# Top-k attention and two MLP layers in one Trainium2 kernel: layers that open with two rows, a 64-token unit moved behind its neighbour, low words of the probabilities made on GpSimd, and one parametric ReLU

## The chip, the core and the metric

The kernel runs on one core of one Trainium2 chip. The metric is the device time of one execution in microseconds (us); lower is better. Durations of single instructions are given in us or, where a row of the trace has them so, in ns. The engines are named as the profile names them: PE (TensorE), DVE (VectorE), ACT (ScalarE), POOL (GpSimd) and SP (the engine that issues most DMAs).

## What is computed

Attention over 4 batches, 8 heads, 576 tokens and 64 channels per head, in which each row of the scores keeps its 32 largest entries, then two MLP layers of 512 to 2048 to 512 channels over all 2304 tokens. Cut to what matters:

```python
scores = (q @ k.T) / 8
kth = np.partition(scores, -32, axis=-1)[..., -32:-31]
scores = np.where(scores >= kth, scores, -1e9)
attn = softmax(scores)                 # 32 entries a row are left
x = (attn @ v).reshape(2304, 512)      # heads side by side
h = np.maximum(x @ w_in1, 0.0);  x = (h * h) @ w_out1
h = x @ w_in2;                   out = np.maximum(0.01 * h, h) @ w_out2
```

## The kernel before, in words

**Numbers.** Most products are made of a high word (the operand rounded to PE's one-pass format, `R`) and a low word (the rest). A layer's hidden row needs 12 matmuls: four channel chunks of high weights by high x, four of high weights by low x, four of low weights by high x. The attention of the first `NATIVE` = 3 units is multiplied in full fp32 instead (line 405, two PE records a matmul); of all later units the probabilities are split in two words.

**Attention.** Two heads are worked on together, a *head pair* (`hp`, 4 of them). `UNITS` (line 27) lists pieces of a batch: (batch, first token, tokens). A unit by a head pair gives score tiles of 128 rows by 576 keys; 144 tiles in all, handled in 72 *pairs of tiles*. The program is written slot by slot, 16 slots to a pair of tiles (loop at line 831): in slots 0 to 13 DVE finds the 32 largest of both tiles, with four MAX8 (line 846) and three MATCH_REPLACE8 (line 848) a tile; around them `at(slot, function)` puts the other steps: loads, scores (line 285, copied from PSUM by ACT in line 286), the exponentials (lines 303 and 307), the normalisation on POOL (line 316), the four transposes of a tile (line 321) and its leftover columns (line 334). `pt_main` (line 318) copies a transposed tile out of PSUM: ACT writes the high word (line 326) and DVE subtracts it from the PSUM tile for the low word (line 327). `av_split` (line 408) multiplies with V, 9 matmuls a head (line 416); `x_out` (line 424) writes x of the MLP as two words. Scores of batches 2 and 3 (`EARLY`) are computed ahead of their turn as filler for PE in the first part, stored to DRAM (`sd`) and loaded back.

**MLP.** The 2304 tokens are cut into `BLOCKS` of 512, 256, 384, 512, 256 and 384. `moe(j, layer)` (line 570) runs one layer of one block in 16 steps `f` of 128 hidden channels: a hidden row of 12 matmuls into the PSUM tile `h`, of which there is one (line 585), the activation, its high word `gh` (ACT) and low word `gl` (POOL, for the last block DVE), and one step later the second product into the `acc` tiles (four of them; lines 635 and 637). The first layer's square takes ACT, ACT and POOL (lines 602 to 604). The second layer's leaky ReLU takes two ACT passes and a POOL subtraction (lines 613 to 615), for the last block one ACT pass and a DVE maximum (lines 609, 610). At the end of a first layer ACT and DVE turn each of the four `acc` tiles into the next layer's x, high word `xh` and low word `xl` (lines 648, 649); the second layer's first row waits for these. At the end of a second layer ACT copies the result to `y`, two buffers, and stores it (lines 652, 654). Layers come in the order (block, layer) 00, 01, 10, 11, 20, 21, 30, 31, 40, 50, 41, 51; weights are read as 64-bit numbers and split into two words during block 0 (`w_convert_steps`, lines 512 to 533), stored to DRAM, and loaded from there by the later blocks.

**What sets the order.** `moe` is a generator. Between attention slots the loop at line 831 lets it run by `rate` quanta, which is a block's number of quanta over the slots until the next block's x is complete (`rslot`, line 773). The framework then orders each engine's instructions by a simulated timeline, in which the attention's functions rank 100 places ahead (`SOON`). On the chip each engine runs its own list in that fixed order.

## Time and profile before

| what | value |
|---|---|
| three runs, median (lowest to highest) | 1200.16 us (1199.25 to 1202.18) |
| the profiled execution, its own time | 1201.19 us |
| its span in the trace | 1199.4 us |
| PE busy | 1130.8 us, 94% |
| DVE busy | 945.1 us, 79% |
| ACT busy | 796.4 us, 66% |
| POOL busy | 678.9 us, 57% |
| DMA traffic | 323.24 MB, mean 270 GB/s |

The span runs from the first to the last instruction; 1.8 us of the profiled execution lie around it. A busy PE is not a PE at its peak, since matmuls are pipelined and their recorded durations overlap; where it matters, distances from start to start are used. PEclk is the clock that was granted to PE as a share of its full 2.4 GHz.

### The profile page before, as it was taken

How to read it: one execution, taken by the hardware profiler on the slowest of the kernel's cores; microseconds unless marked ns; L12 is line 12 of the kernel's file. 1: busy time of each engine (PE TensorE's matmuls, PEld its weight loads, DVE VectorE, ACT ScalarE, POOL GpSimd, SP SyncE). 2: the span in 40 equal slices, each digit the busy share in tenths (PEclk: the TensorE clock that was granted, in tenths of full speed). 3: DMA queues.
4: the chain of work that ended last, by engine and by line, in shares of the span. 5: the costliest groups of instructions: out<-in, count | busy, mean ns of one | idle time of the engine just before them, and what ended most of it. 6: DMA issues, size and time to landing. Idle time of an engine off the chain costs nothing.

```text
span 1199.4 us, 20071 instructions
## 1 busy us (share of the span) xinstructions
PE 1130.8 (94%) x6388; PEld 989.3 (82%) x6388; DVE 945.1 (79%) x1944; ACT 796.4 (66%) x1787; POOL 678.9 (57%) x922
## 2 busy tenths in 40 slices
PE   5899958999899999999998999999999999999997
PEld 4777846887677789988998997888788899998896
DVE  7999999879879899999999999999999910110121
ACT  6999979789889977766656676555666653334322
POOL 7967575778788875467665664555455543005200
PEclk9999988999999999999998999999999999999999
DMA  9868565679889888899987888676677589779973
GB/s 309 277 213 266 201 218 214 234 290 338 305 296 326 281 298 288 282 333 369 326 308 251 283 279 265 206 232 221 203 231 232 184 277 369 249 250 345 353 253 124
DMA packets 105914, 323.24 MB, mean 270 GB/s; under 512 B 16977, under 2 KB 25169, under 8 KB 101713
## 3 DMA queue, kind: packets, MB, share of 16 engines
q1 hardware_dynamic: 103168, 317.24, 77.6%
q10 hardware_dynamic: 2640, 4.72, 1.1%
q8 instruction: 52, 0.85, 0.3%
q14 instruction: 54, 0.43, 0.1%
HBM read 254.54 MB, written 67.37 MB: 268 GB/s over the span
## 4 chain that ended last, share of the span: by engine, by line
PE 69%; ACT 10%; DVE 10%; DMA 5%; POOL 3%; issue 2%; ACTq 0%; SPq 0%; POOLq 0%; DVEq 0%
PE h L592 28%; PE acc L637 14%; PE acc L635 14%; DVE m L846 4%; PE att L416 4%; PE att L321 3%; DVE w L848 3%; PE att L405 2%; DMA wraw<-in_w_dram 2%; ACT e L303 1%; DMA kraw<-in_k_dram 1%; ACT e L307 1%; DMA out_dram<-y 1%; ACT s L286 1%; ACT stage L286 1%
## 5 line engine op out<-in xcount | busy, mean ns | idle before, releaser
L592 PE MATMUL h<-xh,wi 128*128 128x512 f32 (+2 forms) x1280 | 351.8, 347 | 8.6 <-ACT ga L602 3.5
L846 DVE MAX8 m<-w 128x8 f32<-128x576 f32 x432 | 313.6, 747 | 1.3
L592 PEld LDWEIGHTS h<-xh,wi 128*128 128x128 f32 x1280 | 227.3, 191 | 37.1 <-ACT ga L602 5.0
L848 DVE MATCH_REPLACE8 w<-m,w 128x576 f32<-128x576 f32 x288 | 213.5, 743 | 0.8
L592 PE MATMUL h<-xl,wi 128*128 128x512 f32 (+2 forms) x640 | 207.1, 342 | 2.7 <-DVE xl L649 2.6
L618 POOL TENSOR_TENSOR gl<-ga,gh 128x512 fp32r<-128x512 f32 (+2 forms) x160 | 163.0, 1019 | 43.3 <-ACT gh L617 38.9
L635 PE MATMUL acc<-gh,wo 128*128 128x512 f32 (+2 forms) x768 | 157.4, 342 | 0.3 <-ACT y L652 0.3
L637 PE MATMUL acc<-wo,gh 128*128 128x512 f32 x576 | 151.9, 398 | 2.5 <-ACT gh L617 2.5
L615 POOL TENSOR_TENSOR ga<-ga,gb 128x512 f32<-128x512 f32 (+2 forms) x80 | 81.5, 1018 | 122.3 <-ACT gb L614 122.3
L635 PEld LDWEIGHTS acc<-gh,wo 128*128 128x128 f32 x768 | 127.1, 189 | 12.4 <-ACT y L652 0.8
L592 PEld LDWEIGHTS h<-xl,wi 128*128 128x128 f32 x640 | 121.4, 191 | 14.9 <-DVE xl L649 4.3
L303 ACT ACTIVATE e<-s,m 128x576 f32<-128x576 f32 x144 | 112.4, 781 | 31.1 <-DVE m L846 24.2
L637 PEld LDWEIGHTS acc<-wo,gh 128*128 128x128 f32 x576 | 103.9, 188 | 22.9 <-ACT gh L617 4.0
L307 ACT ACTIVATE e<-e,nb 128x576 f32<-128x576 f32 x144 | 110.9, 774 | 5.7 <-POOL nb L297 5.5
L604 POOL TENSOR_TENSOR ga<-ga 128x512 f32<-128x512 f32 (+2 forms) x80 | 66.3, 828 | 82.3 <-ACT gh L603 79.6
L846 DVE MAX8 m<-s 128x8 f32<-128x576 f32 x144 | 103.7, 747 | 7.9 <-ACT s L286 5.9
L848 DVE MATCH_REPLACE8 w<-m,s 128x576 f32<-128x576 f32 x144 | 107.0, 743 | 0.6
L321 PE MATMUL att<-ident,e 128*128 128x128 f32 x576 | 88.1, 279 | 18.1 <-ACT e L307 12.8
L321 PEld LDWEIGHTS att<-ident,e 128*128 128x128 f32 x576 | 69.7, 143 | 31.2 <-ACT e L307 17.4
L602 ACT ACTIVATE ga<-h 128x512 f32<-128x512 f32 (+2 forms) x80 | 39.1, 488 | 80.2 <-PE h L592 77.8
L316 POOL TENSOR_SCALAR e<-e,rc 128x576 f32<-128x576 f32 x108 | 79.7, 751 | 16.6 <-DVE rc L312 15.4
L617 ACT ACTIVATE gh<-ga 128x384 fp32r<-128x384 f32 (+2 forms) x112 | 58.6, 523 | 42.2 <-POOL ga L615 32.2
(94 smaller groups left out, 2133.4 us busy)
## 6 DMA issues: line engine op xcount, KB each, us to landing
wi<-wd SPq DMA_DIRECT2D x160, 512.0 KB, 5.2
wo<-wd SPq DMA_DIRECT2D x160, 512.0 KB, 5.4
wraw<-in_w_dram SPq DMA_DIRECT2D x32, 1024.0 KB, 6.6
sd<-stage SPq DMA_DIRECT2D x72, 288.0 KB, 3.3
s<-sd SPq DMA_DIRECT2D x72, 288.0 KB, 4.6
wd<-wi SPq DMA_DIRECT2D x32, 512.0 KB, 5.6
wd<-wo SPq DMA_DIRECT2D x32, 512.0 KB, 6.0
kraw<-in_k_dram SPq DMA_DIRECT2D x16, 576.0 KB, 4.5
```

The costliest lines, as they stand in the source:

```text
L303: ACT.activation(t["e"], t["s"], AF.Prelu, bias=pr["m8"][:, i, 31:32], scale=-1.0, alpha=1.0 / FAR)
L307: ACT.activation(e, e, AF.Exp, bias=pr["nb"][:, i:i + 1], scale=-FAR, accum_out=pr["sum"][:, i:i + 1])
L316: POOL.tensor_scalar(e, e, pr["rc"][:, i:i + 1], 1.0, op0=OP.mult, op1=OP.mult)
L321: PE.transpose(ps[:, j * P:(j + 1) * P], t["e"][:, j * P:(j + 1) * P], ident)
L592: PE.matmul(h[:, 0:n], lhsT=wi[:, w, c * P:(c + 1) * P], rhs=x[c][y][:, 0:n], start=cnt == 0, stop=cnt == 3 * NK - 1)
L604: POOL.tensor_tensor(a[:, 0:n], a[:, 0:n], a[:, 0:n], op=OP.mult)
L615: POOL.tensor_tensor(a[:, 0:n], a[:, 0:n], b[:, 0:n], op=OP.subtract)
L618: (DVE if j >= GLD else POOL).tensor_tensor(gl[:, 0:n], a[:, 0:n], gh.bitcast(F)[:, 0:n], op=OP.subtract)
L635: PE.matmul(acc[c][:, 0:n], lhsT=wo[:, w, cs], rhs=g[:, 0:n], start=first, stop=last)
L637: PE.matmul(acc[c], lhsT=g[:, cs], rhs=wo[:, w, :], start=first, stop=last)
L846: cur["dve"] = DVE.max(out=m8[:, x, 8 * r:8 * r + 8], in_=t["s"] if r == 0 else t["w"])
L848: cur["dve"] = DVE.match_replace(out=t["w"], in_to_replace=m8[:, x, 8 * r:8 * r + 8], in_values=t["s"] if r == 0 else t["w"], imm_value=NEG)
```

## The change

1. `UNITS` has the 64-token unit (0, 512, 64) behind (1, 0, 256), no longer ahead of it, and `NATIVE` falls from 3 to 2, so that this unit's probabilities are split in two words as well. Block 1 (256 tokens) is then the unit (1, 0, 256) alone, and the rate of block 0's MLP is set by 8 pairs of tiles until block 1 is complete, not 10; that of block 1 by 12, not 10. The scores of the moved unit (`KEPT`) are still computed with its batch, stored to DRAM and loaded back.
2. The low word of a transposed tile is made on POOL: ACT copies the PSUM tile a second time, whole, to `whole` (two buffers), and POOL subtracts the high word from that.
3. A layer opens with two hidden rows at once: at step 0 the 24 matmuls of rows 0 and 1 go out in the order `OPENING`, by the x chunk that they need, the second row into a tile of the `acc` kind; step 1 then has no matmuls of its own. The words `xh` and `xl` at a first layer's end rank 400 places ahead (`SEAM`).
4. The second layer's leaky ReLU is one ACT pass with `Prelu`, for all blocks.

```diff
 UNITS = [
-    (0, 0, 256), (0, 256, 256), (0, 512, 64), (1, 0, 256), (1, 256, 320),
+    (0, 0, 256), (0, 256, 256), (1, 0, 256), (0, 512, 64), (1, 256, 320),
     (2, 0, 256), (3, 0, 256), (2, 256, 320), (3, 256, 320),
 ]
+OPENING = (
+    ((0, 0),), ((1, 0),), ((0, 1),), ((2, 0),), ((1, 1),), ((3, 0),), ((2, 1), (3, 1)),
+)
-NATIVE = 3
+NATIVE = 2
+KEPT = 3
+SEAM = 400
...
         if half == 0:
-            if direct(uh):
+            if direct(uh) and not kept(uh):
                 t["s"] = sbufs[t["i"] % NS]
...
-        if half == 1 and not direct(uh):
+        if half == 1 and (kept(uh) or not direct(uh)):
...
         if split(t["uh"]):
             pts = late["PT"]
             ACT.activation(pts[:, 0:4, c:c + P], x, AF.Copy)
-            DVE.tensor_tensor(pts[:, 4:8, c:c + P], x, pts.bitcast(F)[:, 0:4, c:c + P], op=OP.subtract)
+            whole = late["pool"].tile([P, NJ, P], F, tag="whole", name="whole", bufs=2)
+            ACT.activation(whole, x, AF.Copy)
+            POOL.tensor_tensor(pts[:, 4:8, c:c + P], whole, pts.bitcast(F)[:, 0:4, c:c + P], op=OP.subtract)
...
                 if f == 0:
-                    mm = [(w, c, 0) for w in range(2) for c in range(NK)] + [(0, c, 1) for c in range(NK)]
+                    two = [late["psum"].tile([P, 512], F, tag="acc" if r else "h", name="h", bufs=4 if r else 1)
+                           for r in range(2)]
+                    ws = [wi, wt[si + 1][0]]
+                    mm = [(r, w, c, y) for part in OPENING for r in range(2) for c, y in part
+                          for w in ((0,) if y else (0, 1))]
+                elif f > 1:
+                    two = [late["psum"].tile([P, 512], F, tag="h", name="h", bufs=1)]
+                    ws = [wi]
+                    mm = [(0, 0, c, y) for c in range(NK) for y in range(2)] + [(0, 1, c, 0) for c in range(NK)]
                 else:
-                    mm = [(0, c, y) for c in range(NK) for y in range(2)] + [(1, c, 0) for c in range(NK)]
+                    mm = []
...
-                elif j >= LEAK2:
-                    ACT.activation(a[:, 0:n], h[:, 0:n], AF.Copy, scale=0.01)
-                    DVE.tensor_tensor(a[:, 0:n], a[:, 0:n], h[:, 0:n], op=OP.max)
                 else:
-                    b = late["mlp"].tile([P, 512], F, tag="gb", name="gb", bufs=1)
-                    ACT.activation(a[:, 0:n], h[:, 0:n], AF.Relu)
-                    ACT.activation(b[:, 0:n], h[:, 0:n], AF.Relu, scale=-0.01)
-                    POOL.tensor_tensor(a[:, 0:n], a[:, 0:n], b[:, 0:n], op=OP.subtract)
+                    ACT.activation(a[:, 0:n], h[:, 0:n], AF.Prelu, alpha=0.01)
...
             if layer == 0:
                 xh, xl = x[c]
-                ACT.activation(xh[:, 0:n], acc[c][:, 0:n], AF.Copy)
-                DVE.tensor_tensor(xl[:, 0:n], acc[c][:, 0:n], xh.bitcast(F)[:, 0:n], op=OP.subtract)
+                with tc.high_priority(offset=SEAM):
+                    ACT.activation(xh[:, 0:n], acc[c][:, 0:n], AF.Copy)
+                    DVE.tensor_tensor(xl[:, 0:n], acc[c][:, 0:n], xh.bitcast(F)[:, 0:n], op=OP.subtract)
```

Where the change moves instructions, the built programs show it. First PE at the opening of block 2's second layer (384 tokens; `h` is a hidden row, `xh` and `xl` the two words of x, `PTs` and `VT` the attention's product). Before:

```order
L635 MATMUL acc_7093<-gl_8105,wo_7918 128x384
L592 MATMUL h_8184<-xh0_5146,wi_7998 128x384
L416 MATMUL att_8199<-PTs_3112,VT_7982 128x256 x8
L592 MATMUL h_8184<-xh0_5146,wi_7998 128x384 x7
L416 MATMUL att_8199<-PTs_3112,VT_7982 128x256
L592 MATMUL h_8184<-xl0_5147,wi_7998 128x384 x4
L592 MATMUL h_8230<-xh0_5146,wi_8065 128x384
```

and now:

```order
L656 MATMUL acc_7169<-gl_8213,wo_8034 128x384
L436 MATMUL att_8304<-PTs_2609,VT_8078 128x256
L619 MATMUL h_8292<-xh0_5191,wi_8100 128x384 x4
L436 MATMUL att_8304<-PTs_2609,VT_8078 128x256 x8
L619 MATMUL h_8293<-xh0_5191,wi_8169 128x384 x4
L619 MATMUL h_8292<-xl0_5192,wi_8100 128x384
L619 MATMUL h_8293<-xl0_5192,wi_8169 128x384
L619 MATMUL h_8292<-xh0_5191,wi_8100 128x384 x2
L619 MATMUL h_8293<-xh0_5191,wi_8169 128x384 x2
```

The second row (`h_8293`) now stands inside the first, and the last low words of x are needed 24 row matmuls after the opening began, not 12.

The same place on DVE, where `xl` is made from the `acc` tiles among the MAX and MATCH_REPLACE of the attention. Before:

```order
L649 TENSOR_TENSOR xl0_5147<-acc_7090,xh0_5146 128x384
L649 TENSOR_TENSOR xl0_5147<-acc_7091,xh0_5146 128x384
L846 MAX m8_8369<-s4_105 128x8
L846 MAX m8_8369<-s5_106 128x8
L846 MAX m8_8234<-w_8237 128x8
L649 TENSOR_TENSOR xl0_5147<-acc_7092,xh0_5146 128x384
L649 TENSOR_TENSOR xl0_5147<-acc_7093,xh0_5146 128x384
```

and now:

```order
L671 TENSOR_TENSOR xl0_5192<-acc_7166,xh0_5191 128x384
L867 MAX m8_8325<-w_8328 128x8
L671 TENSOR_TENSOR xl0_5192<-acc_7167,xh0_5191 128x384
L671 TENSOR_TENSOR xl0_5192<-acc_7168,xh0_5191 128x384
L867 MAX m8_8325<-w_8329 128x8
L671 TENSOR_TENSOR xl0_5192<-acc_7169,xh0_5191 128x384
```

Two MAX stand between the first and the last `xl`, not three. Counted over DVE's whole list, the MAX between the last `xl` of block 0 and of block 1, of block 1 and of block 2, of block 2 and of block 3 are 88, 96 and 133 before, and 71, 117 and 139 now.

Last, POOL in block 0's first layer, between the low words of weights (`wi`, `wo`), the square (`ga`) and its low word (`gl`). Before:

```order
L533 TENSOR_TENSOR wi_2862<-wc_2864,wi_2862 128x512
L604 TENSOR_TENSOR ga_2970<-ga_2970 128x512
L533 TENSOR_TENSOR wo_2863<-wc_2864,wo_2863 128x512
L618 TENSOR_TENSOR gl_2969<-ga_2970,gh_2968 128x512
L533 TENSOR_TENSOR wi_2934<-wc_2936,wi_2934 128x512
```

and now:

```order
L553 TENSOR_TENSOR wi_2900<-wc_2902,wi_2900 128x512
L639 TENSOR_TENSOR gl_2925<-ga_2926,gh_2924 128x512
L347 TENSOR_TENSOR PTs_2609<-whole_2982,PTs_2609 128x4x128
L631 TENSOR_TENSOR ga_3000<-ga_3000 128x512
L553 TENSOR_TENSOR wo_2901<-wc_2902,wo_2901 128x512
L639 TENSOR_TENSOR gl_2999<-ga_3000,gh_2998 128x512
L347 TENSOR_TENSOR PTs_2609<-whole_3021,PTs_2609 128x4x128
```

The probabilities' low words (`PTs<-whole`) stand in the queue between the MLP's; 8 of them lie between the first `gl` of layer 00 and the first of layer 01, and 112 in the whole list.

## Rows read from the trace of the kernel before

**Rows 1.** Busy time by stretch, cut at openings (316.24:427.69 is layer 01 alone); columns first.

```profile
core 0: us, PE busy (x) PEld busy (x) DVE busy (x) ACT busy (x) POOL busy (x), PEclk, DMA share, GB/s
200.00:316.24 116.24, 111.15 (x560) 92.14 (x558) 99.48 (x191) 98.43 (x197) 91.26 (x98) 0.99 0.80 287
316.24:427.69 111.45, 106.34 (x505) 85.69 (x505) 98.17 (x186) 101.35 (x195) 94.60 (x98) 0.98 0.89 308
316.24:500.61 184.37, 178.44 (x1075) 155.87 (x1076) 169.99 (x336) 154.79 (x327) 134.80 (x165) 0.99 0.87 299
500.61:645.05 144.44, 142.08 (x906) 134.69 (x904) 142.58 (x302) 91.19 (x214) 93.00 (x140) 1.00 0.91 325
645.05:848.37 203.32, 197.65 (x1007) 168.50 (x1007) 199.27 (x421) 122.89 (x262) 112.60 (x154) 0.97 0.76 247
848.37:1010.18 161.81, 161.18 (x956) 140.64 (x956) 114.10 (x239) 93.86 (x199) 84.68 (x110) 1.00 0.73 243
1010.18:1199.40 189.22, 181.95 (x1022) 169.91 (x1020) 30.20 (x56) 63.37 (x141) 24.81 (x34) 0.99 0.78 266
```

**Rows 2.** Busy time in five openings of layers, from first row to second product.

```profile
645.05:657.83 12.78, 9.86 (x43) 8.58 (x44) 12.72 (x28) 6.77 (x16) 4.75 (x9) 0.73 0.64 225
316.24:327.43 11.19, 9.42 (x30) 6.28 (x31) 11.19 (x23) 10.61 (x20) 7.99 (x9) 0.85 0.98 345
736.16:747.27 11.11, 8.37 (x31) 6.02 (x32) 10.98 (x23) 7.23 (x15) 2.54 (x4) 0.85 0.81 251
848.37:858.23 9.86, 9.27 (x41) 6.61 (x41) 9.79 (x20) 7.84 (x16) 2.85 (x5) 1.00 0.59 188
500.61:507.72 7.11, 6.22 (x43) 5.23 (x41) 7.04 (x17) 4.60 (x13) 2.96 (x4) 1.00 0.82 315
```

**Rows 3.** Timeline of PE, opening of block 2's second layer: start, us, engine, line, operation.

```profile
646.28 1.71 PE L592 MATMUL h<-xh,wi 128*128 128x384 f32 x7
650.40 1.15 PE L592 MATMUL h<-xl,wi 128*128 128x384 f32 x2 [1.95 <-DVE xl L649]
652.52 0.69 PE L592 MATMUL h<-xh,wi 128*128 128x384 f32 x1 [0.96 <-ACT gb L614]
```

**Rows 4.** Timeline of ACT, opening of block 3's first layer.

```profile
742.68 0.60 ACT L652 ACTIVATE y<-acc 128x512 f32<-128x512 f32 x1 [2.58 <-DMA out_dram<-y]
743.70 0.60 ACT L602 ACTIVATE ga<-h 128x512 f32<-128x512 f32 x1 [0.42 <-ACT y L652]
```

**Rows 5.** The chain that ended last, in order of time: start, us, what.

```profile
752.12 2.81 PE acc L635 x12
1031.14 2.08 PE h L592 x12
```

**Rows 6.** Groups of DVE, 500.61 to 645.05: count, busy us, mean ns, idle before.

```profile
L846 DVE MAX8 m<-w 128x8 f32<-128x576 f32 x70 | 50.6, 746 | 0.2
L327 DVE TENSOR_TENSOR PTs<-att,PTs 128x512 fp32r<-128x512 f32 x26 | 17.4, 678 | 0.4 <-ACT PTs L326 0.2
```

**Rows 7.** Groups by shape over the span: the operations that leave, move, or price one.

```profile
L326 ACT ACTIVATE PTs<-att 128x512 fp32r<-128x512 f32 x108 | 62.8, 596 | 19.2 <-PE att L321 18.6
L615 POOL TENSOR_TENSOR ga<-ga,gb 128x512 f32<-128x512 f32 x32 | 41.5, 1298 | 20.4 <-ACT gb L614 20.4
L618 POOL TENSOR_TENSOR gl<-ga,gh 128x512 fp32r<-128x512 f32 x64 | 83.0, 1297 | 15.0 <-ACT gh L617 13.8
L239 POOL TENSOR_TENSOR VT<-vraw,VT 128x320 fp32r<-128x320 f32 x24 | 20.7, 881 | 0.5 <-ACT VT L122 0.5
L405 PE MATMUL att<-PT,VN 128*128 128x64 f32 x64 | 7.8, 275 | 0.0
L405 PE MATMUL att<-PT,VN 64*128 64x64 f32 x16 | 2.6, 284 | 0.0
L416 PE MATMUL att<-PTs,VT 128*128 128x256 f32 x216 | 34.6, 283 | 0.0
L321 PE MATMUL att<-ident,e 128*128 128x128 f32 x576 | 88.1, 279 | 18.1 <-ACT e L307 12.8 <-ACT PT L329 3.0 <-DVE wc L528 1.0
```

More of the change, by code (lines that the diff above doesn't have):

```diff
@@ L74 @@
 )
-LEAK2 = 5
 GLD = 5
@@ L136, in topk_attention_moe_moe2_kernel @@
             n = u["n"]
-            uh = dict(u=u, hp=hp, n=n, b=u["b"], first=(u["t0"] == 0), ti=len(tiles), idx=len(uhs),
+            uh = dict(u=u, hp=hp, n=n, b=u["b"], first=(u["t0"] == 0), i0=u["i"], ti=len(tiles), idx=len(uhs),
                       c0=P * (hp % 2) if n == 64 else 0)
@@ L154, in direct, with kept, score_slot @@
         return uh["b"] not in EARLY
-    for i, uh in enumerate([uh for uh in uhs if direct(uh)]):
+    def kept(uh):
+        return uh["u"]["i"] == KEPT
+    def score_slot(ti):
+        return 16 * (ti // 2) - DLEAD + 5 * (ti % 2)
+    for uh in uhs:
+        uh["zs"] = score_slot(uh["ti"])
+        if kept(uh):
+            ahead_of = [x for x in uhs if x["b"] == uh["b"] and x["hp"] == uh["hp"] and x["i0"] < uh["i0"]][-1]
+            uh["zs"] = score_slot(ahead_of["last"]) + 5
+    in_time = sorted([uh for uh in uhs if direct(uh)], key=lambda uh: uh["zs"])
+    for i, uh in enumerate(in_time):
         uh["di"] = i
@@ L670, in topk_attention_moe_moe2_kernel @@
     order = []
-    for uh in uhs:
+    for uh in in_time + [uh for uh in uhs if not direct(uh)]:
         b, hp, i = uh["b"], uh["hp"], uh.get("di")
-        z = score_slot(uh["ti"])
+        z = uh["zs"]
         if uh["first"] and direct(uh):
@@ L684, in topk_attention_moe_moe2_kernel @@
         if (b, hp) not in vdone or split(uh) and VTB < NHP:
-            assert not uh["u"]["i"] < NATIVE <= units[max(x["i"] for x in units if x["b"] == b)]["i"]
             vdone.add((b, hp))
-            zv = z + DLEAD + 4
+            zv = score_slot(uh["ti"]) + DLEAD + 4
             if split(uh):
@@ L703, in topk_attention_moe_moe2_kernel @@
         used["qraw", i] = z1 + 4
-        used["q", i] = used["KT", b, hp] = score_slot(uh["last"]) + 2
+        used["q", i] = used["KT", b, hp] = (z if kept(uh) else score_slot(uh["last"])) + 2
     later_uhs = {}
@@ L756, in topk_attention_moe_moe2_kernel @@
         for i, t in enumerate(pr["t"]):
-            if direct(t["uh"]):
+            if kept(t["uh"]):
+                at(t["uh"]["zs"], scores, t, 0)
+                at(t["uh"]["zs"] + 2, scores, t, 1)
+            if kept(t["uh"]) or not direct(t["uh"]):
+                at(z - LEAD + i, load_s, t)
+            else:
                 at(z - DLEAD + 5 * i, scores, t, 0)
                 at(z - DLEAD + 2 + 5 * i, scores, t, 1)
-            else:
-                at(z - LEAD + i, load_s, t)
             if i == 0:
```

15 lines of the change are left out of this document (6 added, 9 removed).

## The prediction

> **What bounds the kernel now.** I read busy time by stretch first, cut where the second layers open, since the page's shares mix a first part without an MLP, a middle with both kinds of work and a tail with the MLP alone. The reader is to see that two engines are full at once in the middle [rows 1]: from 500.61 to 645.05 PE is busy for 142.08 of 144.44 us and DVE for 142.58, from 645.05 to 848.37 they have 197.65 and 199.27 of 203.32. From 200 to 316, where weights are also converted, no engine stands out: PE 111.15, DVE 99.48, ACT 98.43, POOL 91.26 of 116.24. After 1010 PE alone is full. So an instruction taken off DVE is worth nothing by itself in the middle; what counts there is where both stand still together, and how each stretch's work divides.
>
> Second, the openings of layers [rows 2], where PE's clock is granted at 0.73 to 0.85 in three of five. The work in them can be counted. A row matmul of 512 columns takes 2.81/12 = 0.234 us from start to start, one of 384 columns 2.08/12 = 0.173 [rows 5], and for 256 columns I take half of 0.234. Transposes take 88.1/576 = 0.153, attention products 34.6/216 = 0.16 [rows 7]. The opening at 645.05 holds 43 matmuls, 24 of them rows: 24 x 0.173 + 19 x 0.155 = 7.1 of 12.78 us, so 5.7 are lost. In the same way 316.24 loses 4.7 (24 rows, 6 others), 736.16 4.7 (21 rows, since 3 came earlier, 10 others), 848.37 1.6 and 500.61 1.4: together 18 us. PE's timeline tells why [rows 3]: it waits 1.95 us for the low words from DVE, then 0.96 us until ACT has emptied the one `h` tile, and then runs matmuls further apart than 0.173. At 736 it is ACT that is late [rows 4]: its third `y` waits 2.58 us for the store of an earlier one to free a buffer, and the first row's activation stands behind that.
>
> **The change, part by part.** I add stretches, each with its own limit, against the profiled execution: 1201.19 us, of which 1.8 lie around the span; it stands 1.0 over the median.
>
> *Two rows.* A layer now starts with 24 matmuls before anything of ACT's is needed, 4.2 us at 384 and 5.6 at 512 columns; the waits of 1.95 and 2.58 us [rows 3, 4] fit under them. What is late next is the first activation: behind the two rows PE has no third one, and waits for ACT's two passes, about 1.2 us at 0.6 each [rows 4], less the last matmuls of the second row, 4 x 0.2. Attention matmuls stand there in most layers, but not in the last four. I leave 1 us lost in each of the first five and add 0.5 for the last four together. Bounds: nothing saved where ACT itself is the late one, all 18 us saved.
>
> *Reordering.* Counted over PE's two lists, the transposed tiles at the start of layers 01, 11, 21 and 31 are 42, 65.6, 90 and 122 before, 41.6, 60, 90 and 124 now: layers 01 and 10 carry 5 tiles less, layers 11 and 20 about 5.5 more. A tile brings PE five transposes and 4.5 products with V, 1.5 us; DVE has seven MAX8 or MATCH_REPLACE8 per tile.
>
> *The moved unit.* Its full-precision products go, 7.8 + 2.6 = 10.4 us [rows 7]; 72 split ones of 64 columns come. The trace has none: a quarter of 0.16 is 0.04, a record of the old form took 10.4/80 = 0.13; I take 0.07, nearer the first since it is the same one-pass form, so 5 us (3 to 9). POOL gets 8 more V splits of 0.88 [rows 7], and SP four more loads and stores of V and of scores, in a stretch where the DMA engines are at 0.80 and 0.89 [rows 1]. I count these transfers at nothing, as they are ordered long before use; without that cover each would cost a few us once.
>
> *Low words and ReLU.* Per tile DVE loses 0.678 [rows 6], ACT gains 0.6, POOL gains what its same-shaped subtraction takes, 1.297 [rows 7]. A step of a second layer gives back one ACT pass and one POOL subtraction, 1.298 at 512 columns [rows 7].
>
> The Trainium skill speaks against this move: "GPSIMD Engine Reference", section "Engine selection", wants elementwise work on the Vector engine, with GpSimd about twice as slow on two inputs. The trace agrees, 1297 against 678 ns. By that rule the low words cost engine time and gain none, which is the first rival below.
>
> Now the stretches.
> - **To 316.2: no change.** Attention's first 16 pairs are as before. Behind them PE loses 10.4 us of products and can do some 2 us of the second row in its early waits; against that ACT gets 10 copies (6 us) and POOL 8 subtractions (10.4), on 98.43 and 91.26 busy of 116.24. Bounds -8 and +13 (below).
> - **316 to 500: 184.4 to 173.8.** PE is the limit. Opening -3.7; 5 tiles -7.5; their 36 direct score matmuls, counted in the lists and priced at 0.16, -5.8; the moved unit's products +5; and -2 for layer 01, where ACT and POOL, now at 91% and 85%, each lose 16 instructions. This makes -14; I take -10.6, since the opening's and ACT's shares overlap.
> - **500 to 645: 144.4 to 155.** DVE is the limit. Its busy time without the 17.4 us of low words [rows 6] is 125.2 for 96 MAX; for the 117 that the new list has there, 152.6; times 144.44/142.58, 155. PE needs less, about 142 + 8.
> - **645 to 848: 203.3 to 197.9.** Openings -(5.7 + 4.7 - 2) = -8.4; two tiles more, +3. DVE drops by 20 us and is no limit.
> - **848 to 1010: 161.8 to 158.4.** Two tiles less, -2.9, opening -0.5.
> - **1010 to the end: 189.2 to 189.7.**
>
> Sum 316.2 + 173.8 + 155 + 197.9 + 158.4 + 189.7 = 1191.0, with 1.8 around it 1192.8: 8.4 less than 1201.2, against the median 1191.8. I say 1192.
>
> **The rivals.** *Block 0's first layer becomes POOL's.* For it: low words of probabilities now queue between those of weights and of `gl`, and POOL was busy for 78.5% of 200 to 316 [rows 1], its gaps being waits for ACT. If it keeps that density, 91.3 + 10.4 = 101.7 us take 129.5, 13.3 more, and everything behind moves: 1205. It decides below a density of 79%, where the loss passes 12 us and the kernel is slower. Against it: in layer 01 POOL runs at 85% and ACT at 91% [rows 1]. Chance 0.14.
>
> *The stall moves instead of leaving.* The two rows end, and PE waits for ACT's passes where it waited for `xl`; in block 2 and 3 ACT's queue has the extra copies in it. If half of the 12.6 us that I take from openings stays, the sum is 1198, no difference that can be measured. For it: half of the opening losses follow waits for ACT [rows 3, 4]. Chance 0.2.
>
> *DVE carries a lead over.* If in the stretch from 500 the attention enters with tiles done ahead, PE's 150 us is the limit, not 155, and if the openings lose nothing, another 5 go: 1182. Against it: the `xl` of both blocks are fixed places in DVE's list, and 117 MAX lie between them. Chance 0.11.
>
> *The change does not do what it says*: the lists show the rows interleaved and the low words on POOL, so only a stall of the second row on its `acc` bank could undo it; that falls under the second rival.
>
> **How the numbers follow.** The forecast, 1184 to 1197 by itself, has 0.55. About 0.3% (3.6 us) is what a measurement of this kernel can tell from no change, so faster is below 1196.6 and slower above 1203.8. Faster: the forecast's 0.51, the third rival's 0.11 and 0.05 of the second, 0.67. Same: 0.04 of the forecast, 0.14 of the second and a little of the first, 0.19. Slower: the rest, 0.14. The range that leaves out 2 in 10 is 1182 to 1205, from the third rival to the first.
>
> **What would show it.** Right: in the five openings the granted clock is 0.95 or more and each lasts 1 us more than its matmuls; DVE is busy for 98% from the last `xl` of block 1 to that of block 2, and for under 90% around it; that stretch lasts about 155 us; PE's total busy time falls by some 15 us. Wrong: layer 00 lasts over 125 us from 200 on with waits for POOL's `gl` or ACT (first rival); PE idles behind the second row, released by `ga` or `gh` (second); PE waits in numbers for `PTs` from POOL, which I count at nothing because ten slots lie between a tile's transposes and its product.

## The result, and the profile after

The changed kernel takes 1189.86 us (median of four runs, 1188.43 to 1190.84), beside 1201.07 us (1199.25 to 1202.18) of the kernel before: a ratio of 0.9907, 95% interval 0.989 to 0.9925. The forecast was 1192, in a range of 1182 to 1205. The profiled execution took 1189.77 us, 1188.0 of them its span.

The page of the changed kernel, busy time of each engine over the span:

```profile
PE 1124.0 (95%) x6376; PEld 985.5 (83%) x6376; DVE 872.1 (73%) x1828; ACT 820.1 (69%) x1823; POOL 744.8 (63%) x958
```

DVE has 73 us less to do than before, ACT 24 and POOL 66 more; PE lost only 6.8 us of busy time.

Busy time by stretch of the changed kernel, cut at the same events as [rows 1]; the second row is layer 01 alone:

```profile
core 0: us, PE busy (x) PEld busy (x) DVE busy (x) ACT busy (x) POOL busy (x), PEclk, DMA share, GB/s
200.00:311.49 111.49, 100.55 (x457) 80.40 (x456) 95.18 (x182) 102.52 (x195) 107.08 (x109) 0.95 0.94 328
311.49:410.91 99.42, 97.87 (x461) 80.20 (x461) 74.31 (x140) 84.27 (x154) 74.44 (x73) 0.99 0.88 323
311.49:486.90 175.41, 172.69 (x1068) 153.48 (x1068) 135.71 (x273) 140.51 (x301) 131.58 (x155) 1.00 0.88 317
486.90:642.08 155.18, 150.26 (x967) 141.80 (x966) 153.71 (x333) 115.99 (x265) 122.45 (x164) 1.00 0.88 306
642.08:840.22 198.14, 194.86 (x1025) 167.63 (x1025) 187.60 (x408) 134.96 (x283) 138.69 (x174) 1.00 0.78 254
840.22:997.88 157.66, 157.27 (x941) 138.57 (x938) 87.58 (x190) 91.63 (x196) 90.26 (x113) 1.00 0.72 246
997.88:1188.00 190.12, 182.10 (x1022) 170.02 (x1020) 21.25 (x40) 58.83 (x125) 12.84 (x18) 0.99 0.78 264
```

The reader is to see where each engine is full. From 486.90 to 642.08 DVE is busy for 99% and holds the stretch, which is longer than before (155.2 for 144.4), because the new order puts more tiles into it. From 642.08 on PE alone is full; DVE has 10.5 us to spare from there to 840 and 70 from 840 to 998. Before 311 POOL is now at 96%, the fullest engine, where it was at 78.5%. And the granted clock, a column near the end, is 1.00 in every stretch from 311 to 998 us (0.99 in layer 01), where before it fell in three openings [rows 2]. Ahead of 311 it is lower than before, 0.95 for 0.99 from 200 us on.

The five openings of [rows 2] in the changed kernel, again from the first row to the second product:

```profile
642.08:651.95 9.87, 9.22 (x55) 8.06 (x55) 9.81 (x24) 5.11 (x12) 3.54 (x6) 1.00 0.87 275
311.49:322.89 11.40, 9.85 (x39) 7.48 (x39) 11.34 (x24) 11.21 (x21) 7.05 (x9) 0.93 1.03 406
727.26:739.65 12.39, 10.81 (x53) 8.66 (x52) 11.26 (x25) 8.73 (x21) 5.67 (x9) 1.00 0.89 279
840.22:851.57 11.35, 10.96 (x56) 8.93 (x54) 11.26 (x24) 9.42 (x21) 6.13 (x9) 1.00 0.59 168
486.90:494.10 7.20, 6.85 (x55) 6.18 (x53) 7.20 (x18) 6.52 (x18) 3.82 (x5) 1.00 0.37 113
```

Each now holds 36 row matmuls, not 24. Priced as in the prediction, the matmuls take 9.2, 8.9, 11.3, 11.5 and 7.2 us; so 0.7, 2.5, 1.1, 0 and 0 us are lost, 4.3 together, for 18 before. These windows begin with the first row, and so leave out a wait that the kernel before does not have: PE stands still ahead of the first row of block 2's second layer until ACT has made `xh`.

```profile
642.08 0.99 PE L619 MATMUL h<-xh,wi 128*128 128x384 f32 x4 [1.70 <-ACT xh L670]
```

With it 6.0 us are lost.

The groups that answer to [rows 6, 7], from the page's fifth part:

```profile
L347 POOL TENSOR_TENSOR PTs<-whole,PTs 128x512 fp32r<-128x512 f32 x112 | 144.6, 1297 | 43.7 <-ACT whole L346 43.2
```

A low word takes 1297 ns on POOL, for 678 on DVE.

### The profile page after: what moved, and what is told of

It reads as the page before. It is cut to its first block, busy times and chain, and to the rows that moved or that the text cites. A ratio compares the mean times of both kernels' runs of the same rounds, so it can differ in the third digit from the quotient of the medians.

```text
span 1188.0 us, 20096 instructions
## 1 busy us (share of the span) xinstructions
PE 1124.0 (95%) x6376; PEld 985.5 (83%) x6376; DVE 872.1 (73%) x1828; ACT 820.1 (69%) x1823; POOL 744.8 (63%) x958
## 4 chain that ended last, share of the span: by engine, by line
PE 57%; DVE 21%; ACT 12%; DMA 5%; issue 2%; POOL 2%; ACTq 0%; SPq 0%; POOLq 0%; DVEq 0%
PE h L619 22%; PE acc L658 13%; DVE m L867 10%; PE acc L656 9%; DVE w L869 8%; PE att L425 3%; PE att L436 3%; PE att L339 3%; ACT e L321 2%; ACT stage L304 1%; PE sp L303 1%; ACT e L325 1%; DMA wraw<-in_w_dram 1%; DMA out_dram<-y 1%; ACT s L304 1%
## 5 line engine op out<-in xcount | busy, mean ns | idle before, releaser
L619 PE MATMUL h<-xh,wi 128*128 128x512 f32 (+2 forms) x1280 | 345.9, 344 | 9.7 <-ACT ga L629 4.5
L619 PE MATMUL h<-xl,wi 128*128 128x512 f32 (+2 forms) x640 | 203.3, 338 | 0.0
L347 POOL TENSOR_TENSOR PTs<-whole,PTs 128x512 fp32r<-128x512 f32 x112 | 144.6, 1297 | 43.7 <-ACT whole L346 43.2
L656 PEld LDWEIGHTS acc<-gh,wo 128*128 128x128 f32 x768 | 127.4, 190 | 13.4 <-ACT y L674 0.7
L639 DVE TENSOR_TENSOR gl<-ga,gh 128x384 fp32r<-128x384 f32 x32 | 17.9, 559 | 152.1 <-ACT gh L638 149.4
L636 ACT ACTIVATE ga<-h 128x512 f32<-128x512 f32 (+2 forms) x96 | 46.6, 491 | 116.3 <-PE h L619 114.8
L334 POOL TENSOR_SCALAR e<-e,rc 128x576 f32<-128x576 f32 x112 | 82.5, 748 | 16.0 <-DVE rc L330 14.5
L656 PE MATMUL acc<-gl,wo 128*128 128x512 f32 (+2 forms) x384 | 88.3, 349 | 3.8 <-POOL gl L639 3.8
```

The source lines that it names most:

```text
L334: POOL.tensor_scalar(e, e, pr["rc"][:, i:i + 1], 1.0, op0=OP.mult, op1=OP.mult)
L347: POOL.tensor_tensor(pts[:, 4:8, c:c + P], whole, pts.bitcast(F)[:, 0:4, c:c + P], op=OP.subtract)
L619: PE.matmul(two[r][:, 0:n], lhsT=ws[r][:, w, c * P:(c + 1) * P], rhs=x[c][y][:, 0:n], start=cnt == mine[0], stop=cnt == mine[-1])
L639: (DVE if j >= GLD else POOL).tensor_tensor(gl[:, 0:n], a[:, 0:n], gh.bitcast(F)[:, 0:n], op=OP.subtract)
L656: PE.matmul(acc[c][:, 0:n], lhsT=wo[:, w, cs], rhs=g[:, 0:n], start=first, stop=last)
```

## The experiments

Twelve kernels ran. "The change" is the kernel above; four take back one part of it, four add a part to the kernel before, and four try to improve on the change. The table gives each one's median and its ratio to the kernel before (run beside it on the same chip), and the stretches of its profiled execution in us: to the first row of layer 01, from there to that of 11, 21 and 31, to layer 50, and the rest. The last column is PE's mean granted clock in that execution, as a share of 2.4 GHz. u_relu's profiled execution is the slowest of its six, so its stretches add up to 6 us more than its median.

| kernel | median | ratio (95%) | to 01 | to 11 | to 21 | to 31 | to 50 | rest | clock |
|---|---|---|---|---|---|---|---|---|---|
| before | 1201.1 | 1 | 316.2 | 184.4 | 144.4 | 203.3 | 161.8 | 189.2 | 0.983 |
| **the change** | 1189.9 | 0.991 (0.989-0.993) | 311.5 | 175.4 | 155.2 | 198.1 | 157.7 | 190.1 | 0.988 |
| u_rows: without two-row openings | 1200.3 | 0.999 (0.998-1.001) | 307.9 | 183.9 | 155.7 | 200.0 | 162.9 | 188.2 | 0.981 |
| u_low: low words on DVE | 1219.2 | 1.015 (1.013-1.017) | 303.3 | 181.6 | 166.2 | 215.8 | 161.4 | 189.5 | 0.968 |
| u_order: old order | 1205.6 | 1.004 (1.002-1.005) | 323.5 | 185.8 | 150.5 | 199.0 | 154.7 | 188.5 | 0.980 |
| u_relu: old leaky ReLU | 1210.4 | 1.008 (1.005-1.011) | 313.7 | 190.6 | 153.5 | 203.2 | 163.6 | 190.1 | 0.983 |
| low_u2: one unit's low words on DVE | 1209.4 | 1.005 (1.003-1.007) | 301.4 | 195.4 | 150.4 | 209.2 | 162.8 | 188.6 | 0.976 |
| d_rows: before + openings | 1211.0 | 1.006 (1.004-1.008) | 327.8 | 185.0 | 144.2 | 200.2 | 162.1 | 190.5 | 0.974 |
| d_rows_not0: the same but for layer 00 | 1201.0 | 0.999 (0.998-1.001) | 317.0 | 185.7 | 142.9 | 202.3 | 159.7 | 190.4 | 0.984 |
| d_low: before + low words on POOL, one-pass ReLU | 1211.6 | 1.008 (1.006-1.010) | 328.4 | 186.4 | 153.3 | 198.4 | 155.2 | 189.2 | 0.982 |
| d_order: before + order | 1232.8 | 1.026 (1.023-1.029) | 304.5 | 187.7 | 154.6 | 231.9 | 162.4 | 188.5 | 0.969 |
| rows_not0: one row in layer 00 | 1194.5 | 0.994 (0.992-0.996) | 307.6 | 177.9 | 155.3 | 200.0 | 160.2 | 188.6 | 0.981 |
| later32: block 1 later | 1205.8 | 1.003 (1.001-1.005) | 318.5 | 195.0 | 147.1 | 195.3 | 160.8 | 188.6 | 0.983 |
| gl_dve3: three gl on DVE | 1196.8 | 0.995 (0.993-0.997) | 315.6 | 177.7 | 151.9 | 199.6 | 160.3 | 188.6 | 0.981 |

Taken back one at a time the parts cost 10.4, 29.4, 15.7 and 20.5 us (medians, against 1189.86; the kernel before took 1201.1 us beside that and 1201.6 and 1202.3 beside these), 76 together, and the change gains 11. Added to the kernel before, which took 1202.35 beside them, openings, low words (with the one-pass ReLU) and order make it 9, 9 and 30 us slower, and the openings behind layer 00 alone gain nothing that can be measured. The parts are not a sum. The runs below say why, as far as they can be followed. One caution goes with all of them: low_u2, rows_not0, later32 and gl_dve3 alter the change by little, were meant to gain, and lose 4.7 to 19.5 us. So what it costs to take a part back holds, beside the part's worth, what a disturbance of this order costs, and a figure of 10 or 15 us cannot be put down to the part alone.

**u_rows.** The two-row branch becomes, for every step:

```diff
-                if f == 0:
-                    two = [late["psum"].tile([P, 512], F, tag="acc" if r else "h", name="h", bufs=4 if r else 1)
-                           for r in range(2)]
-                    ws = [wi, wt[si + 1][0]]
...
+                h = late["psum"].tile([P, 512], F, tag="h", name="h", bufs=1)
+                if f == 0:
+                    mm = [(w, c, 0) for w in range(2) for c in range(NK)] + [(0, c, 1) for c in range(NK)]
+                else:
+                    mm = [(0, c, y) for c in range(NK) for y in range(2)] + [(1, c, 0) for c in range(NK)]
```

> The change without its two-row openings: every layer's second h row is again computed after the first one's whole chain; everything else as in the change. Theory (the openings' waits on PE, some 10 us at each of the five layers that open with both rows waiting, were real time and the two-row opening took most of them): PE idles again at those openings and the time goes back to 1197 to 1202 us. Rival (the openings' waits were slack that the leftover tokens fill or a stretch bound by VectorE hides; the gain came from the other parts): 1189 to 1194 us.

Measured 1200.29: the theory's number, and all of the change's gain. The openings of layers 21 and 31 show the loss, in busy time of two windows of this kernel:

```profile
647.40:660.00 12.60, 12.60 (x59) 11.91 (x60) 12.44 (x27) 9.02 (x21) 6.93 (x10) 0.76 0.64 210
847.35:860.00 12.65, 10.88 (x41) 7.79 (x42) 12.45 (x27) 9.64 (x22) 9.03 (x14) 0.87 0.54 176
```

At 647 PE is busy all the time, yet does its matmuls at a granted clock of 0.76; ahead of it stood a wait of 1.85 us. But the largest loss is not in a second layer: the stretch from layer 01 to 11 is 8.5 us longer, all of it in block 1's first layer. There PE is idle for 4.2 us and not 1.2, has 15 matmuls more, and has lost 3.4 us of full-speed time (a clock of 0.96 over 84.5 us). Its timeline has this wait, and half the clock behind it:

```profile
419.56 0.58 PE L611 MATMUL h<-xh,wi 128*128 128x256 f32 x1 [1.47 <-ACT ga L620]
419.94 0.42 PE L611 MATMUL h<-xl,wi 128*128 128x256 f32 x1
420.16 0.41 PE L611 MATMUL h<-xh,wi 128*128 128x256 f32 x1
```

Rows of 256 columns are 0.21 us apart here, and 0.117 at full clock. By the mean granted clocks of the two profiled executions, 0.981 of 1198.4 and 0.988 of 1188.0 us, 22.8 and 14.3 us of full-speed time were lost, a difference of 8.5. Over all executions of both kernels, 12 and 4, it is 22.6 and 16.6 us: 6.0 of the 10.4 us go with the clock.

**u_low.**

```diff
-            whole = late["pool"].tile([P, NJ, P], F, tag="whole", name="whole", bufs=2)
-            ACT.activation(whole, x, AF.Copy)
-            POOL.tensor_tensor(pts[:, 4:8, c:c + P], whole, pts.bitcast(F)[:, 0:4, c:c + P], op=OP.subtract)
+            DVE.tensor_tensor(pts[:, 4:8, c:c + P], x, pts.bitcast(F)[:, 0:4, c:c + P], op=OP.subtract)
```

> The change with the probabilities' low words computed on VectorE again, straight from the PSUM tile. Theory (a stretch between two second-layer openings lasts as long as the fuller of PE and VectorE; counted over the program, VectorE's work grows to 160 us in the stretch from layer 11 to layer 21 and to 208 us in the one from 21 to 31, where the change's profile shows 155 and 198 us): those two become 162 and 210 us, the sum is 1205 to 1214 us. Rival (VectorE has room, and the whole copies on ScalarE and the low words on GpSimd are what holds layers 00 and 01): 1182 to 1190 us.

Measured 1219.24, 5 us beyond the theory's upper end. Layers 20 and 30 of this kernel:

```profile
545.68:651.16 105.48, 94.92 (x557) 91.47 (x558) 103.45 (x219) 60.49 (x130) 60.29 (x91) 0.92 0.78 262
730.24:866.92 136.68, 122.63 (x581) 101.23 (x580) 132.46 (x280) 74.29 (x155) 62.25 (x86) 0.91 0.64 203
```

DVE is 98 and 97% busy and PE 90%; the two stretches to 21 and 31 are 11 and 18 us longer. This is what the low words on POOL are for: they make the new order possible. The rival's mechanism may be there too: layer 01 starts 8.2 us earlier than in the change (303.3 for 311.5). But this is not the price of ACT's copies and POOL's subtractions, since part of the work has only moved: layer 00 has 14 matmuls fewer, layer 01 has 17 more and lasts 109.9 us, not 99.4. At the start of layer 11 2.0 us are left.

```profile
303.33:413.25 109.92, 104.46 (x478) 84.65 (x478) 87.49 (x162) 89.40 (x161) 72.67 (x72) 0.97 0.91 326
```

**u_order.**

```diff
-    (0, 0, 256), (0, 256, 256), (1, 0, 256), (0, 512, 64), (1, 256, 320),
+    (0, 0, 256), (0, 256, 256), (0, 512, 64), (1, 0, 256), (1, 256, 320),
-NATIVE = 2
+NATIVE = 3
-KEPT = 3
+KEPT = -1
```

> The change with the order of the attention units, the count of natively routed units and the kept unit of the kernel before: the 64 leftover tokens go back to where they were. Theory (moving tokens only moves PE work between stretches: the stretch to layer 01 and the one from 01 to 11 get some 7 and 9 us more of PE's work, the later ones as much less): 1187 to 1194 us, within 0.4% of the change. Rival (the reordering is itself the gain): 1196 to 1201 us.

Measured 1205.56: beyond the rival, slower than the kernel before. The stretches to 01 and 11 are 12.0 and 10.4 us longer, more than counted, and the later ones give back 8.4. Of the first, PE's groups in layer 00 show two causes, here this kernel and then the change:

```profile
L619 PE MATMUL h<-xh,wi 128*128 128x512 f32 x128 | 46.9, 432 | 7.9 <-POOL wi L553 5.4 <-ACT xh L457 1.1 <-ACT ga L629 0.7
L425 PE MATMUL att<-PT,VN 128*128 128x64 f32 (+3 forms) x100 | 17.2, 322 | 0.0
```

```profile
L619 PE MATMUL h<-xh,wi 128*128 128x512 f32 x129 | 45.2, 415 | 2.9 <-ACT ga L629 2.3 <-POOL wi L553 0.3 <-ACT xh L457 0.2
L425 PE MATMUL att<-PT,VN 128*128 128x256 f32 (+1 forms) x20 | 5.2, 394 | 0.0
```

The unit's full-precision products are back, 80 PE records of 12.0 us, and the first rows wait 5.4 us for weights that POOL makes (`wi`). That wait is the next experiment's subject.

**d_rows and d_rows_not0.** The two-row branch of the change and `SEAM` in the kernel before; the second kernel with `if f == 0 and (j, layer) != (0, 0)`.

> The kernel before with the two-row openings and the priority of the openings' words (SEAM) alone. Theory (the openings' waits are real time whatever the rest is): as the change lost 10.4 us without them, the kernel before gains 8 to 11: 1190 to 1193 us. Rival (parts are worth something only together: here VectorE's 194 counted us between the openings of layers 21 and 31, and 139 from 11 to 21, still fill these stretches, so PE's saved waits turn into waits for VectorE): 1195 to 1200 us.

> The kernel before with two-row openings in all layers but 00 (and SEAM). Theory: the openings alone were slower by 0.6% since in layer 00 the second row needs the second step's weights one step earlier, and there GpSimd makes them while it also makes keys of early scores (PE waited 5.5 us for them, and layer 00 lasted 154.9 us against 143.6); with one row there layer 00 ends at 315 to 318 us again, and the gain of the other openings is mostly taken by VectorE (99% busy in layers 10 to 21): 1194 to 1200 us. Rival A (the weights are not the cause, the openings cost something elsewhere): 1207 to 1212 us. Rival B (the other openings are worth their whole 10 us): 1188 to 1192 us.

Measured 1210.98, against both, and 1201.01, 1 us above the theory's range and far from both rivals; layer 01 starts at 317.0 us, as the theory had it, and of the 2 to 8 us of gain that it left nothing shows. In d_rows, PE's timeline at the opening of layer 00, and POOL's:

```profile
172.85 0.63 PE L605 MATMUL h<-xh,wi 128*128 128x512 f32 x1
178.98 1.65 PE L605 MATMUL h<-xh,wi 128*128 128x512 f32 x3 [5.50 <-POOL wi L539]
```

```profile
173.41 1.31 POOL L130 TENSOR_SCALAR KT<-kraw 128x576 fp32r<-128x576 f32 x2 [1.39 <-DMA kraw<-in_k_dram]
174.81 2.77 POOL L253 TENSOR_TENSOR KT<-kraw,KT 64x576 fp32r<-64x576 f32 x2
177.65 1.27 POOL L539 TENSOR_TENSOR wi<-wc,wi 128x512 fp32r<-128x512 f32 x1
```

The second row needs the second step's weights one step sooner. POOL makes them behind keys of early scores that wait for their own load. In the change POOL is free at that place and finishes `wi` 0.9 us after the opening began, not 6.1:

```profile
173.70 1.28 POOL L553 TENSOR_TENSOR wi<-wc,wi 128x512 fp32r<-128x512 f32 x1 [1.19 <-ACT wi L552]
```

So in layer 00 the openings need the new order. Even there they cost: u_rows and rows_not0, with one row in layer 00, reach layer 01 3.6 and 3.9 us sooner than the change. Most of what the wait cost in d_rows is clock: layer 00 lasts 154.92 us at 0.88, of the kernel before 143.58 at 0.94; lost are 18.6 and 8.6 us of full-speed time, 10 of the 11.3. PE's busy time agrees: 138.4 us with 625 matmuls, for 127.4 with 624, and as much idle time. And d_rows_not0 shows that the other openings gain nothing there: the stretches to 21 and 31 are 1.5 and 1.0 us shorter, with DVE 99 and 98% busy in them.

**d_low and d_order.** The same edits as above, on the kernel before; d_low has the one-pass ReLU as well, for room in SBUF.

> The kernel before with the low words made on GpSimd from a whole copy, and the one-pass leaky ReLU that makes room for that copy's buffers; old order, one-row openings. Theory from the change in the old order (which took until 323 us to reach layer 01 and 186 to reach layer 11): VectorE, relieved, lets the attention run ahead into the stretches up to layer 11, where PE is the limit (175.6 counted us of PE's work against 172.7 before), ScalarE's and GpSimd's added passes lengthen layer 00, and what is left is too little PE work at the end: 1202 to 1209 us, slower than before. Rival (VectorE was the limit from layer 11 to 31, so relieving it is a gain by itself): 1188 to 1196 us.

> The change's order alone (the 64 leftover tokens later, two natively routed units, the kept scores) with the old low words on VectorE, old leaky ReLU, one-row openings. Theory (the order takes 9 us of PE's work out of the part before layer 01, and puts work into the stretch from layer 21 to 31 where VectorE then has 223 counted us against 196 before): layer 01 starts near 305 us, that stretch lasts about 230, the sum is 1213 to 1224 us, slower than before. Rival (4.5 us less of PE's work in all, and attention that starts the MLP earlier, is a gain by itself): 1192 to 1198 us.

Measured 1211.62 and 1232.81. Both theories' directions were right, their numbers 3 and 9 us short of it. Without the order, low words on POOL lengthen the part before layer 11 (14 us) and put 9 us more into the stretch to 21: 26 low words leave DVE there, 17.4 us [rows 6], but 114 MAX8 stand in it, not 94, and it is 99% busy again. The two stretches behind give back 12. The one-pass ReLU was not run alone on the kernel before; it changes only second layers, so the 12.2 us of these that lie ahead of layer 01 are the low words'. The order without them overfills DVE; the stretch from 21 to 31 of d_order:

```profile
646.83:878.73 231.90, 208.55 (x1056) 177.49 (x1056) 226.47 (x479) 132.79 (x282) 118.88 (x165) 0.93 0.69 226
```

**u_relu.** The two passes and the subtraction come back; the negative part is written to the tile of `gl`:

```diff
-                else:
-                    ACT.activation(a[:, 0:n], h[:, 0:n], AF.Prelu, alpha=0.01)
+                elif j >= 5:
+                    ACT.activation(a[:, 0:n], h[:, 0:n], AF.Copy, scale=0.01)
+                    DVE.tensor_tensor(a[:, 0:n], a[:, 0:n], h[:, 0:n], op=OP.max)
+                else:
+                    ACT.activation(a[:, 0:n], h[:, 0:n], AF.Relu)
+                    ACT.activation(gl[:, 0:n], h[:, 0:n], AF.Relu, scale=-0.01)
+                    POOL.tensor_tensor(a[:, 0:n], a[:, 0:n], gl.bitcast(F)[:, 0:n], op=OP.subtract)
```

> The change with the old leaky ReLU (two ScalarE passes and a GpSimd subtraction, for the last block a ScalarE pass and a VectorE maximum); the negative part is written to the tile of the low words, so it is rounded to the one-pass format. Theory (in layer 01 ScalarE and GpSimd are the fullest engines, and each gets 16 instructions back; in the other second layers they have room): layer 01 lasts 103 to 110 us and not 99, the stretch between the openings of layers 21 and 31 gains 2 to 4 us from VectorE's maxima and shifted tiles, the sum is 1192 to 1198 us. Rival (they hide): 1188 to 1191 us.

Measured 1210.39 (1206.95 to 1216.41), 12 us beyond the theory. The place was right: layer 01 lasts 114.4 us, not 99.4. PE's groups there, of this kernel and of the change:

```profile
L619 PE MATMUL h<-xh,wi 128*128 128x512 f32 x129 | 43.7, 405 | 2.9 <-ACT gl L640 2.6 <-DVE xl L676 0.3
L663 PE MATMUL acc<-wo,gh 128*128 128x512 f32 x120 | 32.9, 416 | 6.9 <-ACT gh L643 6.9
```

```profile
L619 PE MATMUL h<-xh,wi 128*128 128x512 f32 x128 | 42.6, 402 | 1.6 <-ACT ga L636 1.1 <-DVE xl L671 0.4
L658 PE MATMUL acc<-wo,gh 128*128 128x512 f32 x120 | 30.9, 396 | 0.0
```

and of the kernel before, which has the two passes and the subtraction too, with a tile of their own:

```profile
L592 PE MATMUL h<-xh,wi 128*128 128x512 f32 x129 | 44.4, 406 | 2.9 <-ACT gb L614 1.8 <-ACT wi L532 0.9 <-ACT xh L648 0.2
L637 PE MATMUL acc<-wo,gh 128*128 128x512 f32 x120 | 31.3, 401 | 1.6 <-ACT gh L617 1.6
```

In u_relu the high word, which goes through ACT, ACT, POOL and ACT again, comes too late for the second product, 6.9 us of waits; the one pass takes POOL out of that way. But the same way costs the kernel before only 1.6 us, and behind its second pass PE waits 1.8 us, where it waits 2.6 in u_relu. So the passes alone do not make the 15 us. Beside the order and the openings, u_relu differs from the kernel before in the tile shared with `gl` (ACT waits 5.1 us over the span for PE to have read it, though not in layer 01) and in the low words in POOL's list; which of these it is, and how much of the 20.5 us is the ReLU's, stays open.

**Four tries to beat the change.** low_u2 makes the low words of unit (1, 0, 256) on DVE; rows_not0 leaves layer 00 its one row; later32 moves block 1's start by `rslot[1] += 32`; gl_dve3 adds `or (j, layer) == (0, 0) and f < 3` to the condition that puts `gl` on DVE.

> The change with the low words back on VectorE for one unit alone, (1, 0, 256), whose tiles lie in layers 00 and 01; all other low words stay on GpSimd. Theory (in layer 00 every step waits for ScalarE and GpSimd, 0.90 and 0.87 busy, and there the whole copies and the subtractions on GpSimd cost some 8 us, as the run with all low words on VectorE reached layer 01 at 303 us and not 311; VectorE has room there): layer 01 starts at 303 to 306 us, the two stretches from 11 to 31 give or take 3 us, the sum is 1182 to 1187 us. Rival (layer 00 is shortened only because its attention work is put off, and returns later): 1188 to 1192 us.

> The change with one row in the opening of layer 00 alone. Theory (layer 00 was 4 us shorter in the run without two-row openings; the other openings keep theirs): layer 01 starts at 307 to 308 us, the rest as in the change, 1184 to 1188 us, faster than both kernels. Rival (the schedule behind it shifts, counted 6 tiles' worth of VectorE's work less before layer 01 and 8 us more between the openings of 21 and 31; and a wait of 1.5 us at one place lets PE's clock fall): 1190 to 1200 us.

> The change with block 1's first layer, and with it the rate mark, placed two pairs of attention tiles later: some 10 us of VectorE's work leave the stretch from layer 11 to layer 21, which VectorE fills to 99% in the change's profile, for earlier stretches that PE bounds. Theory (that stretch is VectorE's; relieved, it falls from 155 to PE's own 143 to 149 us, while the stretch before it grows by 4 us with the PE work that it takes over): 1184 to 1188 us. Rival (PE's work only moves, and the waits with it): 1189 to 1192 us.

> The change with gl, the low word of the activation, made on VectorE and not on GpSimd in the first three steps of layer 00. In the change's profile GpSimd makes two low words of probabilities (2.52 us) right ahead of the first gl, PE waits 2.72 us for it at 204.65 and then runs at half its clock until 210: some 5 to 6 us. Theory (the low words' price on GpSimd is this place, and the waits' price is paid mostly in clock): PE's wait there falls to about 1 us or less, the low clock behind it goes, layer 01 starts at 306 to 308 us; behind it the counted work per stretch is within 4 us of the change's, so 1182 to 1187 us. Rival (as in the other kernels that differ from the change in one thing, another wait opens elsewhere and the clock falls there): 1189 to 1200 us.

All four miss, at 1209.36, 1194.51, 1205.77 and 1196.78; in the second and the fourth the rival held, in the others neither. None beats the change. What was meant to get shorter mostly did: low_u2 and rows_not0 reach layer 01 at 301.4 and 307.6 us, later32's stretch to 21 falls to 147.1. Part of what was not foreseen is in what no list of counted work describes, a wait of a few us and PE's clock after it. In low_u2 it can be followed. First ACT's timeline of that kernel, then PE's, then busy time in windows of 2 us:

```profile
414.64 0.60 ACT L677 ACTIVATE y<-acc 128x512 f32<-128x512 f32 x1 [1.55 <-DMA out_dram<-y]
415.13 0.59 ACT L344 ACTIVATE PTs<-att 128x512 fp32r<-128x512 f32 x1
415.61 0.60 ACT L349 ACTIVATE whole<-att 128x512 f32<-128x512 f32 x1
```

```profile
416.27 0.53 PE L303 MATMUL att<-KT,q 128*128 128x288 f32 x2 [1.81 <-ACT whole L349]
```

```profile
412.00:414.00 2.00, 2.00 (x21) 2.00 (x19) 1.27 (x4) 1.07 (x3) 1.92 (x4) 1.00 0.90 236
414.00:416.00 2.00, 0.46 (x4) 0.22 (x2) 1.93 (x5) 1.36 (x3) 0.69 (x1) 1.00 0.73 291
416.00:418.00 2.00, 1.73 (x11) 1.59 (x11) 1.15 (x2) 2.00 (x6) 1.71 (x2) 0.79 0.99 304
418.00:420.00 2.00, 2.00 (x11) 2.00 (x11) 1.38 (x3) 2.00 (x5) 1.50 (x2) 0.50 0.94 355
...
432.00:434.00 2.00, 2.00 (x11) 2.00 (x10) 0.00 (x0) 0.34 (x2) 0.74 (x2) 0.50 0.56 113
434.00:436.00 2.00, 2.00 (x18) 2.00 (x17) 0.00 (x0) 0.22 (x2) 0.32 (x1) 0.95 0.90 275
```

ACT's copy to `y` stands ahead of the attention's copies in its list and waits for an earlier store to free one of two buffers, as in [rows 4]; PE waits 1.81 us for the PSUM tile behind it, and then runs with a granted clock of 0.50 (1.2 GHz) from 417 to 434. Layer 10 lasts 86.25 us at a mean of 0.90: 8.6 us of full-speed time, of the 10.3 by which it is longer than in the change. There the third and the fourth copy to `y` wait for a store as well, 1.41 and 0.71 us, but later, when PE has other work: it waits 0.54 us behind ACT in all, and keeps its clock. The third copy:

```profile
422.35 0.60 ACT L674 ACTIVATE y<-acc 128x512 f32<-128x512 f32 x1 [1.41 <-DMA out_dram<-y]
```

Another 9.8 us of low_u2's loss are in layer 01, 109.2 us with 16 matmuls more, in part the rival's mechanism, work put off from layer 00. The 11.1 us that its stretch to 31 is longer were not followed. later32 waits 5.49 us for weights at 431 in layer 01, which lasts 119.7 us with 35 matmuls more and has lost 6.8 us by the clock. And gl_dve3 shows the wait that it was made against, and the one that it got; first the change, then gl_dve3, PE's timeline of both:

```profile
204.65 2.07 PE L656 MATMUL acc<-gl,wo 128*128 128x512 f32 x4 [2.72 <-POOL gl L639]
```

```profile
204.30 1.20 PE L656 MATMUL acc<-gl,wo 128*128 128x512 f32 x4 [2.14 <-DVE gl L639]
...
246.26 0.50 PE L619 MATMUL h<-xh,wi 128*128 128x512 f32 x1 [3.62 <-ACT wi L552]
```

In the change the four products last 2.07 us, at half clock; in gl_dve3 1.20, but the clock falls behind them all the same (0.61 from 206 to 210 us). The wait is little shorter, since `gl` begins on DVE only 0.7 us sooner than on POOL and lasts 1.67 us there, where the next one takes 0.67:

```profile
202.58 1.67 DVE L639 TENSOR_TENSOR gl<-ga,gh 128x512 fp32r<-128x512 f32 x1
```

And the wait for weights at 246 is one that the change does not have.

## Why the prediction was right, and where its steps failed

**The stretches behind layer 01.** Forecast 173.8, 155, 197.9, 158.4 and 189.7 us, measured 175.4, 155.2, 198.1, 157.7 and 190.1. With 4.7 us less than forecast before layer 01, the sum comes out 3.0 us short. The rule that made the second, a stretch of DVE's lasts as long as DVE's work in it, held in every run: in layers 11 and 20 DVE is 98 or 99% busy in all of the kernels, from 142.9 us of stretch to 166.2, and DVE's forecast work of 152.6 us measured 153.7. That an instruction taken off DVE is worth nothing by itself there fits d_low, where other work of DVE's came into the room.

The other numbers are better than their working. From layer 01 to 11 the terms add up to -14, and 3.4 us were taken off for an overlap of the opening with ACT's 2 us, which cannot be more than 2; that the forecast came within 1.6 us is in part luck. PE was the limit there, as said: in layer 01 it has 461 matmuls for 505, 97.9 us of work for 106.3, and is idle for 1.6 us, not 5.1. From layer 21 to 31 DVE was to drop by 20 us, to under 90%. It dropped by 11.7, to 95%: the two tiles that the stretch gains were priced for PE and not for DVE, where at seven operations of 0.746 us each they make 10.4. PE was still the fuller engine, by 7.3 us.

**"To 316.2: no change."** This step failed, by 4.7 us, within its bounds of -8 and +13. It set the moved unit's products against added copies and subtractions and took them to cancel. Layer 00 before, and now (columns as in [rows 1]):

```profile
172.66:316.24 143.58, 127.41 (x624) 103.65 (x623) 126.27 (x246) 119.28 (x237) 105.43 (x114) 0.94 0.76 272
174.12:311.49 137.37, 121.89 (x546) 95.13 (x545) 120.99 (x235) 123.25 (x238) 119.94 (x125) 0.95 0.88 309
```

PE's busy time fell by 5.5 us, and its idle time did not grow (16.2 and 15.5), though POOL has 14.5 us more to do and ACT 4.0: the added work found room. Run alone, the parts do cancel: to layer 01 the order takes off 11.7 us (d_order) and the low words add 12.2 (d_low). The openings, alone, add 11.5 (d_rows). Together they make -4.7. The second row's weights, and the keys that u_order and d_rows show ahead of them on POOL, were not in the sum at all; with the new order they cost little (a wait of 0.28 us).

**The openings.** The total was nearly right (12.6 us taken, 10.4 lost again in u_rows; in the five openings 4.3 us left for 5 forecast, 6.0 with the wait ahead of 642), its places were not: 3.7, 8.4 and 0.5 us were forecast in the stretches to 11, 31 and 50, and u_rows lost 8.5, 1.8 and 5.2 there, and won 5.5 back in layer 00 and in the last layers. The step that failed is the count of lost time, made from the matmuls of five openings alone: a first layer (10) whose wait the kernel before does not have was left out. Nor does a layer start with 24 matmuls "before anything of ACT's is needed": the first rows need `xh`, which ACT makes, and at 642 us PE waits 1.70 us for it. Of the signs named, the granted clock was 0.95 or more in four of the five openings; in layer 01's it was 0.93, with 2.5 us lost.

**The leaky ReLU.** Priced at -2 us in layer 01 by its engine time. u_relu gives 15 there, in its slowest execution and with more than the ReLU changed. In the kernel before PE waits 1.8 us for the second pass and 1.6 for the high word in layer 01, 3.4 together, and in the change 1.1 for the one pass and nothing for the high word. By these waits the term was of the right size; whether the new order makes it larger stays open.

**"PE's total busy time falls by some 15 us."** It fell by 6.8. The figure had no working of its own.

**The rivals.** *POOL's layer 00*: POOL did not keep its 79%; from 200 us on it went to 96%, and layer 00 got shorter with it. A price is there in the old order, 12.2 us (d_low); in the new one it was outweighed. *The stall moves*: it would have left half of the openings' loss; a quarter is left, a third with the wait ahead of 642. The largest rests are ACT's, as it said (1.15 us at 320, 1.70 at 642, 1.58 at 736). For `PTs` from POOL, which the prediction counted at nothing, PE waits once, 0.5 us. *DVE's lead*: the stretch from 11 to 21 has 155.2 us, no lead.

**The rule on GpSimd.** The Trainium skill, "GPSIMD Engine Reference", section "Engine selection", holds as a price (1297 ns for 678) and, in d_low, as advice: in the old order the move, with the one-pass ReLU, is slower by 0.8%. With the new order the measurement decides the other way: going back to DVE costs 29 us. Neither the openings, nor the low words with the ReLU, nor the order would have been kept on a test by itself.
